# A linear-attention and feed-forward kernel on one core: its opening section in written order, and loads of k, r and v that no longer wait for one another

## The chip, the core and the metric

The kernel runs on one core of a Trainium2 chip. A core has five engines with instruction queues of their own: TensorE (PE in the profile; PEld is its loading of weights), VectorE (DVE), ScalarE (ACT), GpSimd (POOL) and SyncE (SP), which in this kernel issues nearly all DMA transfers. Engines wait for one another and for DMAs by semaphores. The metric is the device time of one execution, in microseconds (us); lower is better. A change counts as faster or slower from 2% on, which is 10.4 us here.

## The reference: what is computed

Two blocks, one after the other, in float32. The first is a recurrent attention (RWKV-5) with batch 4, 8 heads, 768 steps and head size 48; the second is a feed-forward block whose two branches are multiplied.

```python
def _attn_ref(r, k, v, w, u):
    B, H, S, D = r.shape                       # 4, 8, 768, 48
    state = np.zeros((B, H, D, D), dtype=np.float32)
    y = np.zeros_like(r)
    for t in range(S):
        kt, vt, rt = (k[:, :, t], v[:, :, t], r[:, :, t])
        cur = np.einsum('bhd,bhe->bhde', u[None] * kt, vt)
        y[:, :, t] = np.einsum('bhd,bhde->bhe', rt, state + cur)
        state = w[None, :, :, None] * state + np.einsum('bhd,bhe->bhde', kt, vt)
    return y

def _moe_ref(x, w1, w2, w3, w_out):            # x (3072, 384), d_ff 1024
    a = x @ w1
    b = x @ w2
    h = a * b @ w3
    return h @ w_out
```

w is a decay between 0.85 and 0.95 for each head and channel. The weights w1, w2, w3 and w_out arrive in float64, 8 bytes a number, and the kernel turns them into float32 itself.

## The kernel before

The sequence is cut into 6 chunks of 128 steps. A chunk of one batch entry is a *unit*; there are 24, numbered from 0. Inside a chunk the recurrence becomes matrix products, for which k and r are scaled by powers of w. A short section ahead, the *prologue*, computes those powers and a flag: if every w lies between 0.6 and 1.6, a fast arm is taken, otherwise a careful one. All engines load the flag and branch. With these inputs it is the fast arm.

In the fast arm the order of the instructions on TensorE, ScalarE, VectorE and SyncE is a written list. Its words are a letter for the step and numbers for the unit or the piece of weights:

```python
ORDER = """
kr.2 v.2 d.0 W.2 N.0 e.0 f.0 M.0 k.0 g.0 H.0 U.0 kr.3 d.1 T.0 k.1 L.0 R.0 e.1 kr.4 t.0 i.0 f.1 r.0 T.1 W.3 Q.0 p.0 A.0
M.1 h.1 j.0 S.0 t.1 d.2 R.1 k.2 m.0 r.1 R.2 kr.5 e.2 U.1 N.1 r.2 f.2 A.1 M.2 H.1 T.2 i.1 L.1 m.1 V.0 d.3 p.1 W.4 Q.1
...
"""
```

`kr.n` and `v.n` issue the loads of unit n, `W.i` that of the weight piece i. `d`, `e` and `f` form the products k*r*u and sum them; `k` scales k and r; `M`, `N`, `H`, `L` and `Q` turn a weight piece into float32, by turns on ScalarE and VectorE; `T`, `R`, `t` and `r` turn k and r on TensorE and copy them; `U` and `A` are products for the state and inside the chunk; `S`, `V` and `Y` make the output of a unit; `a`, `b`, `c` and `u` are the first layer of the feed-forward block.

The loads. k, r and v are small pieces of 192 KB, in rows of 192 bytes; a weight piece `W` has 768 KB. There are three buffers for each. Every small piece waits for the small piece two before it:

```python
small = []

def load(n, which="krv"):
    ...
    for nm, src, dst in (("k", k, krin[n % NIN][:, 0]), ("r", r, krin[n % NIN][:, 1]), ("v", v, vnat[n % NV][:, :, :D])):
        if nm in which:
            small.append(nc.sync.dma_start(out=dst, in_=src[b, :, ts, :].rearrange("h t d -> t h d")))
            if len(small) > 2:
                tc.add_manual_dep(small[-1].ins, small[-3].ins.name, ONE_AFTER_THE_OTHER, reason="few small pieces at a time")

def fetch(i, queue=nc.sync):
    if i < len(pieces):
        _, m, n = pieces[i].shape
        landed[i] = raws[i % NRAW][:, :m * n].rearrange("p (m n) -> p m n", m=m)
        queue.dma_start(out=landed[i], in_=pieces[i])
```

The prologue. Its order on the engines is chosen by a scheduler, not by the list. w is loaded twice: as one row for the flag, and by channels, in two halves, for the powers. The powers `both` have a buffer of their own, whose memory the fast arm uses again:

```python
nc.sync.dma_start(out=wrow, in_=w.rearrange("h d -> (h d)").rearrange("(o n) -> o n", o=1))
for i in range(2):
    nc.sync.dma_start(out=wucol[i * PAD:i * PAD + D], in_=w.rearrange("(p i) (d o) -> i d p o", i=2, o=1)[i])
load(0, "kr")
fetch(0)
nc.sync.dma_start(out=ub..., in_=u...)
load(0, "v")
load(1, "kr")
fetch(1)
load(1, "v")

nc.vector.tensor_reduce(ends[:, 0:1], wrow, AX.X, ALU.min)
nc.vector.tensor_reduce(ends[:, 1:2], wrow, AX.X, ALU.max)
nc.vector.tensor_scalar(ends[:, 2:3], ends[:, 0:1], W_LOW, None, ALU.is_ge)
nc.vector.scalar_tensor_tensor(flag, ends[:, 1:2], W_HIGH, ends[:, 2:3], ALU.is_le, ALU.mult)

# powers of w by doubling: wn_in, then both, on VectorE
...
for g in range(2):
    nc.vector.tensor_copy(out=both[:, g, :, T:], in_=both[:, g, :, :T])
    ps = psW.tile([P, NP, C], F32, tag="w", name=f"ps_p{g}")
    for p in range(NP):
        nc.tensor.transpose(ps[:, p, :], both[:, g, p, :], ident)
    nc.scalar.copy(out=pn_in[:, g].rearrange("t h d -> t (h d)"), in_=ps.rearrange("x p t -> x (p t)"))

inside = nc.values_load(flag[0:1, 0:1], min_val=0, max_val=1, ...)
```

First steps of the fast arm, to which the profile's line numbers 408, 411, 415 and 399 belong:

```python
def scale(n):                                   # k.n
    nc.vector.tensor_mul(krs[n % NS][:, :, :, :D], krin[n % NIN], pn[:, :, :, :D])
def rk(n):                                      # d.n
    ruk[n] = work.tile([C, H, D], F32, tag="ruk", bufs=1, name=f"ruk{n}")
    nc.vector.tensor_mul(ruk[n], krin[n % NIN][:, 0], krin[n % NIN][:, 1])
def rku(n):                                     # e.n
    nc.vector.tensor_mul(ruk[n], ruk[n], ub)
def dots(n):                                    # f.n
    nc.vector.tensor_reduce(dg[n], ruk[n], AX.X, ALU.add)
```

Of the kernel before, what the change touches and what calls it, by code (L numbers as in the profile page):

```python
# [8 lines left out]
F32 = mybir.dt.float32  # L9
# [8 lines left out]
ONE_AFTER_THE_OTHER = mybir.DependencyInfo(mybir.DependencyClass.Sync, mybir.DependencyReason.DATA)  # L18
# [5 lines left out]
kr.2 v.2 d.0 W.2 N.0 e.0 f.0 M.0 k.0 g.0 H.0 U.0 kr.3 d.1 T.0 k.1 L.0 R.0 e.1 kr.4 t.0 i.0 f.1 r.0 T.1 W.3 Q.0 p.0 A.0  # L24
M.1 h.1 j.0 S.0 t.1 d.2 R.1 k.2 m.0 r.1 R.2 kr.5 e.2 U.1 N.1 r.2 f.2 A.1 M.2 H.1 T.2 i.1 L.1 m.1 V.0 d.3 p.1 W.4 Q.1
v.3 Y.0 t.2 j.1 S.1 g.2 N.2 A.2 k.3 V.1 H.2 R.3 kr.6 Y.1 U.2 m.2 M.3 v.4 T.3 N.3 L.2 a.0.0.0 k.4 r.3 W.5 i.2 a.0.1.0
H.3 p.2 c.0.0.0 e.3 L.3 R.4 j.2 S.2 f.3 M.4 W.6 U.3 Q.3 b.0.0.0 o.4 h.3 c.0.1.0 i.3 t.3 V.2 d.4 p.3 k.5 kr.7 T.4 Y.2
e.4 A.3 v.5 r.4 x.5 S.3 t.4 b.0.1.0 m.3 o.5 y.5 j.3 M.5 V.3 u.0.0.0 u.0.1.0 U.4 f.4 Y.3 v.6 A.4 Q.2 g.4 a.0.0.1 k.6
N.5 b.0.0.1 M.6 N.6 m.4 c.0.0.1 H.6 a.0.1.1 z.5 u.0.0.1 L.6 H.5 b.0.1.1 c.0.1.1 x.6 W.9 L.5 a.0.2.2 u.0.1.1 y.6 i.4
W.8 l.5 Q.6 p.4 d.5 a.0.3.2 Q.5 c.0.2.2 kr.8 j.4 N.4 e.5 S.4 H.4 c.0.3.2 M.8 z.6 U.5 f.5 M.9 V.4 N.8 d.6 L.4 A.5 i.5  # L30
kr.9 b.0.2.2 Y.4 h.5 o.6 e.6 W.7 p.5 m.5 v.7 l.6 Q.4 b.0.3.2 j.5 u.0.2.2 N.9 k.7 U.6 f.6 A.6 x.7 g.6 S.5 k.8 y.7 V.5
d.7 M.7 a.0.4.2 m.6 v.8 kr.10 o.7 e.7 u.0.3.2 Y.5 f.7 z.7 x.8 b.0.4.2 c.0.4.2 d.8 y.8 h.7 kr.11 e.8 i.6 a.0.5.2 f.8
p.6 u.0.4.2 l.7 d.9 j.6 b.0.5.2 c.0.5.2 e.9 H.8 f.9 L.8 H.9 W.11 d.10 L.9 A.7 Q.8 W.12 U.7 u.0.5.2 a.0.6.2 N.7 i.7 H.7
p.7 k.9 L.7 a.0.7.2 j.7 kr.12 c.0.6.2 x.9 W.10 Q.9 y.9 S.6 Q.7 c.0.7.2 z.8 o.8 V.6 m.7 e.10 b.0.6.2 Y.6 g.8 v.9 N.10
N.11 S.7 M.10 f.10 M.11 u.0.6.2 z.9 V.7 o.9 H.10 b.0.7.2 l.8 d.11 Y.7 H.11 v.10 L.10 e.11 L.11 Q.10 W.13 g.9 Q.11 W.14
a.1.0.2 N.12 u.0.7.2 M.12 f.11 H.12 M.13 a.1.1.2 d.12 L.12 N.13 e.12 c.1.0.2 W.15 Q.12 M.14 H.13 N.14 L.13 b.1.0.2
H.14 c.1.1.2 W.16 Q.13 L.14 Q.14 W.17 M.15 N.15 b.1.1.2 H.15 u.1.0.2 L.15 Q.15 W.18 M.16 N.16 A.8 H.16 u.1.1.2 a.1.2.2
L.16 m.8 l.9 W.19 N.17 M.17 Q.16 H.17 M.18 b.1.2.2 N.18 c.1.2.2 H.18 L.17 L.18 Q.17 W.20 M.19 Q.18 W.21 G.0.0 N.19
G.0.1 K.0.0 u.1.2.2 U.8 H.19 a.1.3.2 K.0.1 i.8 L.19 k.10 p.8 W.22 M.20 N.20 kr.13 x.10 F.0 c.1.3.2 H.20 M.21 y.10 j.8
L.20 Q.19 W.23 M.22 Q.20 N.21 N.22 H.21 H.22 L.21 b.1.3.2 X.0 Q.21 W.24 L.22 Q.22 W.25 M.23 N.23 A.9 u.1.3.2 U.9 H.23  # L40
S.8 i.9 L.23 z.10 V.8 k.11 o.10 a.1.4.2 g.10 N.24 x.11 v.11 kr.14 Q.23 Y.8 m.9 y.11 b.1.4.2 p.9 W.26 N.25 f.12 c.1.4.2
j.9 l.10 d.13 e.13 S.9 u.1.4.2 o.11 A.10 z.11 a.1.5.2 m.10 a.1.6.2 c.1.5.2 l.11 a.1.7.2 c.1.6.2 b.1.5.2 V.9 u.1.5.2
U.10 c.1.7.2 v.12 G.1.0 i.10 Y.9 G.1.1 g.11 k.12 b.1.6.2 x.12 kr.15 p.10 f.13 y.12 K.1.0 d.14 b.1.7.2 M.24 j.10 M.25
e.14 u.1.6.2 K.1.1 H.24 S.10 H.25 L.24 z.12 A.11 u.1.7.2 o.12 U.11 Q.24 L.25 V.10 m.11 W.28 G.2.0 k.13 g.12 W.27 G.2.1
v.13 F.1 i.11 kr.16 Q.25 p.11 f.14 N.26 Y.10 j.11 l.12 d.15 K.2.0 x.13 K.2.1 e.15 y.13 N.27 G.3.0 X.1 U.12 S.11 k.14
o.13 V.11 i.12 kr.17 A.12 Y.11 x.14 G.3.1 v.14 g.13 a.2.0.2 z.13 m.12 K.3.0 f.15 y.14 p.12 d.16 G.4.0 K.3.1 e.16
b.2.0.2 j.12 K.4.0 c.2.0.2 l.13 U.13 u.2.0.2 S.12 k.15 z.14 o.14 V.12 i.13 A.13 Y.12 x.15 G.4.1 g.14 v.15 F.2 m.13
y.15 kr.18 K.4.1 f.16 l.14 d.17 M.26 e.17 M.27 H.26 p.13 H.27 L.26 j.13 S.13 L.27 W.29 Q.26 M.28 W.30 V.13 Q.27 o.15
z.15 N.28 A.14 Y.13 H.28 U.14 X.2 m.14 G.5.0 L.28 v.16 G.5.1 i.14 g.15 F.3 W.31 Q.28 N.29 k.16 M.29 f.17 kr.19 p.14
H.29 j.14 L.29 x.16 l.15 Q.29 S.14 y.16 K.5.0 N.30 d.18 X.3 F.4 K.5.1 N.31 e.18 o.16 z.16 G.6.0 X.4 G.6.1 K.6.0 F.5  # L50
M.30 K.6.1 H.30 M.31 L.30 H.31 Q.30 L.31 s.1.2.0 Q.31 s.1.2.1 F.6 s.1.0.0 X.5 s.1.2.3 s.1.1.0 s.1.3.0 s.1.1.2 s.1.3.1
s.1.1.1 s.1.3.3 s.1.3.2 s.1.0.1 s.1.0.2 s.1.0.3 s.1.2.2 G.7.0 X.6 s.1.1.3 U.15 K.7.0 G.7.1 i.15 P.0.0.0 K.7.1 k.17
p.15 F.7 x.17 kr.20 j.15 y.17 A.15 X.7 s.0.1.0 V.14 s.0.0.0 E.0.0.0 l.16 B.0 P.0.1.0 Y.14 v.17 s.0.0.1 g.16 m.15
a.2.1.2 s.0.0.3 B.1 E.0.1.0 f.18 B.2 a.2.2.2 c.2.1.2 B.3 s.0.1.2 s.0.0.2 s.0.2.0 b.2.1.2 d.19 c.2.2.2 s.0.2.2 s.0.2.1
s.0.1.1 s.0.2.3 s.0.3.0 b.2.2.2 s.0.1.3 s.0.3.1 u.2.1.2 s.0.3.3 e.19 s.0.3.2 P.0.0.2 u.2.2.2 P.0.1.2 E.0.0.2 P.0.0.3
E.0.1.2 P.0.0.4 E.0.0.3 P.0.1.3 E.0.0.4 P.0.0.5 E.0.1.3 P.0.1.5 E.0.0.6 E.0.0.5 D.0.0.0 P.0.1.4 E.0.1.6 A.16 E.0.1.4
U.16 E.0.1.5 m.16 D.0.1.0 P.0.0.6 i.16 k.18 p.16 P.0.0.1 j.16 kr.21 S.15 x.18 z.17 o.17 V.15 E.0.0.1 E.0.0.7 U.17 Y.15
a.2.3.2 i.17 g.17 y.18 v.18 k.19 D.0.0.1 kr.22 p.17 f.19 a.2.4.2 l.17 d.20 j.17 c.2.3.2 x.19 e.20 y.19 P.0.1.1 c.2.4.2
# [4 lines left out]
v.19 k.20 p.18 f.20 kr.23 x.20 l.18 a.2.6.2 c.2.5.2 j.18 y.20 d.21 e.21 b.2.5.2 c.2.6.2 a.2.7.2 u.2.5.2 s.2.1.0  # L63
# [25 lines left out]

# [4 lines left out]
def kernel(  # L94
# [86 lines left out]
    wucol = const.tile([P, NP, 1], F32)  # L181
    nc.vector.memset(wucol, 1.0)
    warm = const.tile([1, 1], F32)
    nc.vector.memset(warm, 0.0)
    nc.scalar.activation(out=warm, in_=warm, func=ABS)
# [13 lines left out]
    small = []  # L199

    def load(n, which="krv"):

        if n >= NU:
            return
        c, b = units[n]
        ts = slice(c * C, (c + 1) * C)
        for nm, src, dst in (("k", k, krin[n % NIN][:, 0]), ("r", r, krin[n % NIN][:, 1]), ("v", v, vnat[n % NV][:, :, :D])):
            if nm in which:
                small.append(nc.sync.dma_start(out=dst, in_=src[b, :, ts, :].rearrange("h t d -> t h d")))
                if len(small) > 2:  # L210
                    tc.add_manual_dep(small[-1].ins, small[-3].ins.name, ONE_AFTER_THE_OTHER, reason="few small pieces at a time")

# [19 lines left out]
    wrow = const.tile([1, DM], F32)  # L232
    ub = const.tile([P, H, D], F32)
    nc.sync.dma_start(out=wrow, in_=w.rearrange("h d -> (h d)").rearrange("(o n) -> o n", o=1))
    for i in range(2):
        nc.sync.dma_start(out=wucol[i * PAD:i * PAD + D], in_=w.rearrange("(p i) (d o) -> i d p o", i=2, o=1)[i])
    load(0, "kr")
    fetch(0)
    nc.sync.dma_start(out=ub.rearrange("t h d -> t (h d)"),
                      in_=u.rearrange("h d -> (h d)").rearrange("(o n) -> o n", o=1).to_broadcast([P, DM]))  # L240
    load(0, "v")
    load(1, "kr")
    fetch(1)
    load(1, "v")


    ends = const.tile([1, 3], F32)
    flag = const.tile([1, 1], I32)
    nc.vector.tensor_reduce(ends[:, 0:1], wrow, AX.X, ALU.min)
    nc.vector.tensor_reduce(ends[:, 1:2], wrow, AX.X, ALU.max)  # L250
    nc.vector.tensor_scalar(ends[:, 2:3], ends[:, 0:1], W_LOW, None, ALU.is_ge)
    nc.vector.scalar_tensor_tensor(flag, ends[:, 1:2], W_HIGH, ends[:, 2:3], ALU.is_le, ALU.mult)


    pn_in = const.tile([C, 2, H, PAD], F32)
    with tc.tile_pool(name="once", bufs=1) as once, tc.tile_pool(name="psW", bufs=2, space=PSUM) as psW:

        wn_in = const.tile([P, LEVELS + 1, 3 * NP, 1], F32)
        nc.vector.tensor_scalar(wn_in[:, 0, 0:NP, :], wucol, W_LOW, W_HIGH, ALU.max, ALU.min)
        for l in range(LEVELS):  # L260
            nc.vector.tensor_mul(wn_in[:, l + 1, 0:NP, :], wn_in[:, l, 0:NP, :], wn_in[:, l, 0:NP, :])
        nc.vector.reciprocal(wn_in[:, 0:LEVELS, NP:2 * NP, :], wn_in[:, 0:LEVELS, 0:NP, :])
        nc.vector.tensor_copy(out=wn_in[:, 0:LEVELS, 2 * NP:, :], in_=wn_in[:, 0:LEVELS, 0:NP, :])

        both = once.tile([P, 2, NP, C], F32)
        nc.vector.memset(both[:, 0, :, HT:HT + 1], 1.0)
        nc.vector.tensor_copy(out=both[:, 1, :, HT:HT + 1], in_=wn_in[:, 0, NP:2 * NP, :])
        bf = both.rearrange("x g p t -> x (g p) t")
# [8 lines left out]
        for g in range(2):  # L277
            nc.vector.tensor_copy(out=both[:, g, :, T:], in_=both[:, g, :, :T])
            ps = psW.tile([P, NP, C], F32, tag="w", name=f"ps_p{g}")
            for p in range(NP):  # L280
                nc.tensor.transpose(ps[:, p, :], both[:, g, p, :], ident)
            nc.scalar.copy(out=pn_in[:, g].rearrange("t h d -> t (h d)"), in_=ps.rearrange("x p t -> x (p t)"))
# [594 lines left out]
```

## Time and profile before

| | |
|---|---|
| time, median of 3 | 519.57 us (519.14 to 519.92) |
| span of the profiled execution | 517.4 us |
| TensorE busy | 492.6 us (95%) |
| VectorE, ScalarE, GpSimd busy | 278.4, 182.6, 6.0 us |
| moved by DMA | 52.72 MB, in 96865 packets, 77729 of them under 512 bytes |

The profile comes from one execution. It has a picture of the span in 40 slices, in which a digit is the busy share in tenths; groups of instructions, with the time that their engine sat idle before them and who ended that idle time; the chain of work that ended last, followed back from the end, at each step to what released it; and the instructions in order of time. Names such as `raw<-in_moe_w_dram` say what is written and what is read: `raw` are the weight pieces, `krin` holds k and r of a unit, `vnat` v, `krs` the scaled k and r, `ps_p` the turned powers, `tt` the turned r, `ps_a` and `ps_b` products. `L408` is a line of the kernel. Matmuls overlap in TensorE's pipeline, and the ends shown for them are modelled.

### The profile page before, as it was taken

To read this page: it belongs to the slowest core of one execution; us is meant where nothing else is said; L and a number is where in the kernel's file an instruction comes from. 1 tells how busy PE (TensorE), PEld (TensorE's weight loads), DVE (VectorE), ACT (ScalarE), POOL (GpSimd) and SP (SyncE) were. 2 spreads that over 40 slices of the span, in tenths; PEclk is the share of its full clock that TensorE was granted. 3 is DMA by queue.
4 is the path that set the end of the run, shared out by engine and by line. 5 is a ranking of instruction groups with operands and counts; after the bars stand their busy time and mean duration, and the time that the engine had idled before them with its cause. 6 is when DMAs were issued, how large, how long until landed. Compare 5 with 4: busy or idle time off the path is not lost.

```text
span 517.4 us, 12199 instructions
## 1 busy us (share of the span) xinstructions
PE 492.6 (95%) x5192; PEld 321.8 (62%) x5192; DVE 278.4 (54%) x587; ACT 182.6 (35%) x455; POOL 6.0 (1%) x23
## 2 busy tenths in 40 slices
PE   1969999999999999999999999999999999999996
PEld 1757544445466566759797477564874754855486
DVE  6888798788475686575424542376321314211342
ACT  3677546766467483411302200340051410001100
POOL 4000000000000000000000000000000000000000
PEclk9999999999999999999999999999999999999999
DMA  7788887668537592301601301220041100000001
GB/s 204 165 220 241 210 219 209 168 232 252 157 94 198 153 232 69 75 3 50 182 32 45 95 0 46 63 79 32 0 129 42 48 1 0 7 24 16 1 16 67
DMA packets 96865, 52.72 MB, mean 102 GB/s; under 512 B 77729, under 2 KB 88226, under 8 KB 96802
## 3 DMA queue, kind: packets, MB, share of 16 engines
q1 hardware_dynamic: 96802, 51.86, 36.9%
q8 instruction: 43, 0.70, 0.6%
q14 instruction: 20, 0.16, 0.1%
HBM read 39.65 MB, written 12.19 MB: 100 GB/s over the span
## 4 chain that ended last, share of the span: by engine, by line
PE 75%; DMA 13%; ACT 4%; DVE 4%; SPq 2%; issue 1%; ACTq 0%; DVEq 0%
PE ps_a L659 20%; PE ps_b L659 19%; DMA raw<-in_moe_w_dram 6%; PE ps_w L387 6%; DMA tt<-scratch 3%; PE ps_s4b L716 3%; PE ps_a12b L716 3%; PE ps_a22t L716 3%; PE ps_s2t L716 3%; PE ps_s1t L716 3%; PE ps_s3t L716 3%; PE ps_a11b L716 3%; PE ps_y L619 2%; SPq L480 2%; PE ps_a L519 2%; PE ps_y L633 2%
## 5 line engine op out<-in xcount | busy, mean ns | idle before, releaser
L659 PE MATMUL ps_a<-xT,w 128*128 128x512 f32 (+1 forms) x300 | 131.4, 581 | 0.8 <-ACT xT L641 0.7
L659 PE MATMUL ps_b<-xT,w 128*128 128x512 f32 (+1 forms) x300 | 131.1, 578 | 0.9 <-DVE abt L670 0.5
L659 PEld LDWEIGHTS ps_b<-xT,w 128*128 128x128 f32 x300 | 55.9, 190 | 63.7 <-issue 56.9
L670 DVE TENSOR_TENSOR abt<-ps_b,a 128x512 f32<-128x512 f32 (+1 forms) x50 | 33.3, 666 | 110.2 <-PE ps_b L659 110.1
L659 PEld LDWEIGHTS ps_a<-xT,w 128*128 128x128 f32 x300 | 55.3, 190 | 57.8 <-issue 53.6
L665 ACT COPY a<-ps_a 128x512 f32<-128x512 f32 (+1 forms) x50 | 28.2, 566 | 127.1 <-PE ps_a L659 123.3
L544 ACT COPY wide<-st 64x192 f32<-64x192 f32 x88 | 30.5, 347 | 56.5 <-PE ps_y L619 27.6
L426 ACT ACTIVATE AT<-same,dg 128x64 f32<-128x64 f32 x160 | 40.4, 336 | 6.2 <-DVE dg L415 3.8
L387 PE MATMUL ps_w<-wo,w3T 128*128 128x384 f32 x128 | 42.5, 487 | 0.0
L387 PEld LDWEIGHTS ps_w<-wo,w3T 128*128 128x128 f32 x128 | 23.9, 190 | 15.7 <-ACT wide L544 0.2
L361 ACT ACTIVATE t<-raw 128x512 uint32<-128x512 uint32 (+2 forms) x32 | 22.4, 705 | 7.2 <-DVE w3n L357 5.0
L619 PEld LDWEIGHTS ps_y<-tt,wide 128*32 128x32 f32 x1056 | 16.5, 111 | 11.2 <-issue 5.6
L399 DVE TENSOR_TENSOR krs<-krin,pn_in 128x768 f32<-128x768 f32 x24 | 22.8, 949 | 0.0
L619 PE MATMUL ps_y<-tt,wide 128*32 128x64 f32 x1056 | 21.1, 223 | 1.7 <-ACT xT L641 1.0
L633 PE MATMUL ps_y<-AT,vnat 64*64 64x64 f32 x1152 | 22.3, 223 | 0.0
L468 DVE STREAM_TRANSPOSE tr<-krs 128x768 f32<-128x768 f32 x19 | 18.5, 973 | 6.5 <-DMA scratch<-tr 6.4
L512 PE MATMUL ps_a<-vnat,krs 64*64 64x48 f32 x704 | 16.7, 227 | 5.1 <-DVE krs L399 3.3
L633 PEld LDWEIGHTS ps_y<-AT,vnat 64*64 64x64 f32 x1152 | 19.3, 136 | 3.1 <-issue 1.4
L485 ACT COPY kT<-tt 128x512 f32<-128x512 f32 x19 | 11.7, 617 | 26.9 <-DMA tt<-scratch 23.8
L547 DVE COPY_PREDICATED AT<-later,ps_a 128x512 f32<-128x512 int32 x24 | 17.4, 726 | 5.6 <-PE ps_a L519 3.0
L519 PEld LDWEIGHTS ps_a<-tt,kT 64*64 64x64 f32 x768 | 14.9, 141 | 8.8 <-issue 4.3
L512 PEld LDWEIGHTS ps_a<-vnat,krs 64*64 64x64 f32 x704 | 14.3, 142 | 9.4 <-issue 8.8
(102 smaller groups left out, 564.2 us busy)
## 6 DMA issues: line engine op xcount, KB each, us to landing
raw<-in_moe_w_dram SPq DMA_DIRECT2D x16, 512.0 KB, 4.9
scratch<-tr SPq DMA_DIRECT2D x19, 384.0 KB, 3.4
raw<-in_moe_w_dram SPq DMA_DIRECT2D x8, 768.0 KB, 6.4
tt<-scratch SPq DMA_DIRECT2D x38, 128.0 KB, 3.2
krin<-in_k_dram SPq DMA_DIRECT2D x24, 192.0 KB, 3.3
krin<-in_r_dram SPq DMA_DIRECT2D x24, 192.0 KB, 3.4
vnat<-in_v_dram SPq DMA_DIRECT2D x24, 192.0 KB, 4.0
raw<-in_moe_w_out_dram SPq DMA_DIRECT2D x8, 384.0 KB, 4.4
```

What stands on the lines that cost most here:

```text
L387: nc.tensor.matmul(ps, lhsT=w3T[j][:, kc, :], rhs=wo[kc], start=(kc == 0), stop=(kc == KF - 1))
L399: nc.vector.tensor_mul(krs[n % NS][:, :, :, :D], kr, pn[:, :, :, :D])
L426: nc.scalar.activation(out=AT[n][:, i, p, :], in_=same, func=COPY, scale=dg[n][:, h:h + 1])
L512: nc.tensor.matmul(added(n)[rows(i), a, p, :], lhsT=kk[rows(a), 2 * p + i, :], rhs=vnat[n % NV][rows(a), 2 * p + i, 0:D], start=True, stop ...
L519: nc.tensor.matmul(upper(n)[rows(a), i, p, :], lhsT=kT[n][rows(i), p, rows(a)], rhs=rT[n][rows(i), p, 2 * a:2 * a + 2], start=True, stop=True)
L544: nc.scalar.copy(out=wide[a][n % 2][rows(i), :, i * D:(i + 1) * D], in_=st[units[n][1]][rows(i)])
L619: nc.tensor.matmul(yt[n][g * Q:(g + 1) * Q, a, q, :], lhsT=wide[a][n % 2][:, p, j * Q:(j + 1) * Q], rhs=rw[:, p, 2 * a:2 * a + 2] if fast ...
L633: nc.tensor.matmul(yt[n][rows(g), a, q, :], lhsT=vv[rows(a), x:x + PAD], rhs=AT[n][rows(a), h % 2, h // 2, :], start=(a, g) not in seen, s ...
L659: nc.tensor.matmul(ps, lhsT=(w1 if x == "a" else w2)[:, z, q, js], rhs=xT[c][:, q, ts], start=(q == 0), stop=(q == KM - 1))
L665: nc.scalar.copy(out=a, in_=ps)
L670: nc.vector.tensor_mul(abt[c, j][:, parts_of_tokens[part]], factor["b", c, j, part], factor["sa", c, j, part])
L716: nc.tensor.matmul(ps, lhsT=of[:, m * C:(m + 1) * C], rhs=w34[:, KH * (x == 1) + j, :DH] if x < 2 else made[b][:, j, :], start=(j == 0), s ...
```

## The change

The prologue is written in the order in which the engines are to run it, and reorganised:

- w is loaded once, by channels; its two halves are issued by SyncE and by ScalarE. The load of v goes ahead of that of u.
- The flag is no longer made from the smallest and largest w. Each w is compared with its value held between the bounds; a product with ones on TensorE counts the differences, and VectorE sums the four counts and tests for zero, at the end of the prologue.
- The powers `both` lie in the third weight buffer, `raws[2]`, in place of a buffer of their own. The third weight piece, W.2, which goes into that buffer, follows after them.
- One of the two copies of powers moves from VectorE to ScalarE.
- 14 products of a matrix of ones keep TensorE busy while it has nothing else to do; their result is not used.
- The loads of k, r and v lose the wait for the piece two before. In the list, `kr.n` becomes `kk.n rr.n`, the same two loads in the same order.

```diff
-ONE_AFTER_THE_OTHER = mybir.DependencyInfo(mybir.DependencyClass.Sync, mybir.DependencyReason.DATA)
...
-kr.2 v.2 d.0 W.2 N.0 e.0 f.0 M.0 k.0 g.0 H.0 U.0 kr.3 d.1 T.0 k.1 L.0 R.0 e.1 kr.4 t.0 i.0 f.1 r.0 T.1 W.3 Q.0 p.0 A.0
+kk.2 rr.2 v.2 d.0 W.2 N.0 e.0 f.0 M.0 k.0 g.0 H.0 U.0 kk.3 rr.3 d.1 T.0 k.1 L.0 R.0 e.1 kk.4 rr.4 t.0 i.0 f.1 r.0 T.1
...
-                small.append(nc.sync.dma_start(out=dst, in_=src[b, :, ts, :].rearrange("h t d -> t h d")))
-                if len(small) > 2:
-                    tc.add_manual_dep(small[-1].ins, small[-3].ins.name, ONE_AFTER_THE_OTHER, reason="few small pieces at a time")
+                nc.sync.dma_start(out=dst, in_=src[b, :, ts, :].rearrange("h t d -> t h d"))
...
-    nc.sync.dma_start(out=wrow, in_=w.rearrange("h d -> (h d)").rearrange("(o n) -> o n", o=1))
-    for i in range(2):
-        nc.sync.dma_start(out=wucol[i * PAD:i * PAD + D], in_=w.rearrange("(p i) (d o) -> i d p o", i=2, o=1)[i])
-    load(0, "kr")
-    fetch(0)
-    nc.sync.dma_start(out=ub.rearrange("t h d -> t (h d)"),
-                      in_=u.rearrange("h d -> (h d)").rearrange("(o n) -> o n", o=1).to_broadcast([P, DM]))
-    load(0, "v")
...
-    nc.vector.tensor_reduce(ends[:, 0:1], wrow, AX.X, ALU.min)
-    nc.vector.tensor_reduce(ends[:, 1:2], wrow, AX.X, ALU.max)
-    nc.vector.tensor_scalar(ends[:, 2:3], ends[:, 0:1], W_LOW, None, ALU.is_ge)
-    nc.vector.scalar_tensor_tensor(flag, ends[:, 1:2], W_HIGH, ends[:, 2:3], ALU.is_le, ALU.mult)
...
+    with tc.manual_schedule(engines={PE, ACT, DVE, SP}), tc.tile_pool(name="psW", bufs=2, space=PSUM) as psW:
+        nc.vector.memset(wucol, 1.0)
+        for i, queue in enumerate((nc.sync, nc.scalar)):
+            queue.dma_start(out=wucol[i * PAD:i * PAD + D], in_=w.rearrange("(p i) (d o) -> i d p o", i=2, o=1)[i])
+        load(0, "kr")
+        fetch(0)
+        load(0, "v")
+        nc.sync.dma_start(out=ub.rearrange("t h d -> t (h d)"),
+                          in_=u.rearrange("h d -> (h d)").rearrange("(o n) -> o n", o=1).to_broadcast([P, DM]))
+        load(1, "kr")
+        fetch(1)
+        load(1, "v")
+
+        busy = pn_in[:, 0].rearrange("t h d -> t (h d)")[:, :C]
+        nc.vector.memset(busy, 1.0)
...
+        keep_busy(14)
...
+        both = raws[2].bitcast(F32)[:, :2 * NP * C].rearrange("x (g p t) -> x g p t", g=2, p=NP)
...
             nc.vector.tensor_mul(wn_in[:, l + 1, 0:NP, :], wn_in[:, l, 0:NP, :], wn_in[:, l, 0:NP, :])
+            if l == 0:
+                nc.vector.tensor_tensor(outs[:, 0:NP], wn_in[:, 0, 0:NP, 0], wucol[:, :, 0], ALU.not_equal)
+                ps_out = psW.tile([1, NP], F32, tag="out", bufs=1, name="ps_out")
+                nc.tensor.matmul(ps_out, lhsT=outs[:, NP:NP + 1], rhs=outs[:, 0:NP], start=True, stop=True)
...
-        both = once.tile([P, 2, NP, C], F32)
...
+        nc.vector.tensor_copy(out=both[:, 0, :, T:], in_=both[:, 0, :, :T])
+        nc.scalar.copy(out=both[:, 1, :, T:], in_=both[:, 1, :, :T])
+        nc.vector.tensor_reduce(outs[0:1, NP + 1:], ps_out, AX.X, ALU.add)
+        nc.vector.tensor_scalar(flag, outs[0:1, NP + 1:], 0.0, None, ALU.is_equal)
         for g in range(2):
-            nc.vector.tensor_copy(out=both[:, g, :, T:], in_=both[:, g, :, :T])
             ps = psW.tile([P, NP, C], F32, tag="w", name=f"ps_p{g}")
```

## The prediction

> **What bounds the kernel now.** I read the page's slices first, then the busy time by stage, then the chain that ended last, and last the instructions of the first 40 us in order of time. The slices (one is 12.9 us):
>
> ```profile
> PE   1969999999999999999999999999999999999996
> ...
> DMA  7788887668537592301601301220041100000001
> ```
>
> TensorE is full from the fourth slice to the last but one; the DMA engines are nearly full only in the first seven. So the kernel is TensorE-bound except at its head. The stages put numbers on that (us, then busy us and instruction counts of PE, PEld, DVE, ACT and POOL, the granted clock, the DMA share, GB/s):
>
> ```profile
> 0.00:9.60 9.60, 1.94 (x8) 1.57 (x8) 4.96 (x30) 2.10 (x4) 6.04 (x23) 1.00 0.71 177
> 9.60:26.00 16.40, 12.15 (x224) 9.81 (x224) 14.22 (x26) 10.75 (x23) 0.00 (x0) 1.00 0.78 188
> 26.00:39.00 13.00, 9.11 (x221) 7.57 (x222) 11.05 (x21) 10.27 (x25) 0.00 (x0) 1.00 0.88 221
> 39.00:48.00 9.00, 8.33 (x238) 6.83 (x237) 7.52 (x14) 5.99 (x18) 0.00 (x0) 1.00 0.91 255
> ...
> 58.00:104.00 46.00, 45.05 (x631) 23.50 (x631) 40.49 (x82) 28.00 (x72) 0.00 (x0) 1.00 0.76 198
> ...
> 200.00:400.00 200.00, 199.51 (x1747) 137.54 (x1745) 92.69 (x204) 46.16 (x130) 0.00 (x0) 1.00 0.20 56
> ```
>
> TensorE idles 7.66 + 4.25 + 3.89 = 15.8 us of the first 39, and 24.8 us of the whole span, of which 4.1 lie in the drain after 510 us. From 39 to 510 us there are 4.9 us in all. Whatever the change does must be read from the first 39 us: if the list of instructions gets to that point sooner by x, the end comes sooner by about x.
>
> What sets the pace up to there is in the chain that ended last (start, length, what):
>
> ```profile
> 4.82 5.47 DMA vnat<-in_v_dram
> ...
> 10.35 4.13 DMA krin<-in_r_dram
> ...
> 14.50 2.64 DMA krin<-in_k_dram
> ...
> 17.57 6.42 DMA raw<-in_moe_w_dram
> ...
> 25.81 6.45 DMA raw<-in_moe_w_dram
> ...
> 38.35 6.32 DMA raw<-in_moe_w_dram
> ```
>
> Each of the first three starts within 0.1 us of the landing of the piece two places before it: that is the wait "few small pieces at a time". It holds the one SyncE queue, so the third weight piece behind it is issued only at 17.57 us. VectorE, 84 to 87% busy in each stage from 9.6 to 48 us, shows what this costs it:
>
> ```profile
> 9.63 0.56 DVE L408 TENSOR_TENSOR ruk<-krin 128x384 f32<-128x384 f32 x1 [1.98 <-PE ps_p L281]
> ...
> 14.60 0.56 DVE L408 TENSOR_TENSOR ruk<-krin 128x384 f32<-128x384 f32 x1 [1.16 <-DMA krin<-in_r_dram]
> ...
> 25.49 0.56 DVE L408 TENSOR_TENSOR ruk<-krin 128x384 f32<-128x384 f32 x1 [0.59 <-DMA krin<-in_r_dram]
> ...
> 32.28 0.56 DVE L354 TENSOR_SCALAR t<-raw 128x768 uint32<-128x768 uint32 x1 [1.17 <-DMA raw<-in_moe_w_dram]
> ```
>
> The last numbers are its idle time before the instruction and who ended it: once TensorE's transposes of the powers, three times a load.
>
> **What the Trainium skill says.** "DMA: Bandwidth & Descriptors", section "Why small descriptors are slow (HBM only)": each packet carries a fixed cost. The trace agrees: while the 192-byte pieces of k and r run (3.5 to 5.5 us) about 200 GB/s flow, while a weight piece or u runs about 360. Same page, "Latency and other measured facts": loading a register from memory costs at least about 600 ns. Here ScalarE's last copy of the prologue is dispatched at 9.57 us and its first instruction past the branch starts at 10.26, so load and branch together fit in 0.69 us. Same page, "Issuing engines are not separate DMA queues": two issuing engines save only issue time. No run shows it yet. "TensorE: Matmul & The Clock Gate", Part 1: some 3.4 us of activity should bring the full clock. The trace agrees only in part: four transposes take 1.11 us at 13.9 us and 0.66 at 29.0, so the array is at half clock and then at full, but it stays at half for 12 us of work with gaps of at most 0.7 us. So small products and transposes may hardly count as activity.
>
> **The change part by part.** The order of instructions past the branch is the same on TensorE, ScalarE, VectorE and SyncE; "kk, rr" in the list is what "kr" was, and the new list words are not used. What differs there are waits: VectorE's first instruction no longer waits for TensorE, the third weight piece waits for the prologue's readers of its buffer, and every wait of a small load for the one two before it is gone. The wait of each DMA for the one eight before it stays.
>
> 1. *Prologue on VectorE.* Its chain starts when w has landed, at 3.58 us. The first half of w is issued at 1.21 us behind the row of w, the second at 1.61. Now the row is gone and the halves go out side by side: done about 0.65 us sooner, chain start 2.9. The chain lasted to 7.64, or 4.06 us. One comparison comes in (0.15), one of two copies of 0.25 goes to ScalarE, and the flag's sum and test come at the end (two tiny instructions, 0.4 with their waits). Flag at 2.9 + 4.06 + 0.15 - 0.25 + 0.4 = 7.25. With 0.7 for load and branch VectorE enters the list at 7.95 instead of 9.63: 1.7 us.
>
> 2. *First loads.* Service times from the rates: a 197 KB small piece 1.0 us, a 786 KB weight piece 2.2, u 0.55; landing 1.0 after the last byte (checked on the first v: data from 3.5, 5.75 us of pieces, 9.25 + 1.0 against 10.29 seen). k starts 0.73 earlier, data from 2.75. In the new order k, r, weights, v, u, k, r, weights, v, then k, r, v, weights: u lands at 9.5, the second r at 11.5, the third r at 16.7, the third weight piece at 19.9 (seen now: 23.99). After it k, r, k, r: the fourth r at 21.9 (now 25.46), the fourth weight piece at 26.1 (now 32.25). Of the 1.7 us only 1.1 survives, because the product with u (10.57 now) waits for u, which has moved behind v.
>
> 3. *VectorE down the list.* k and r of the second unit are there before it needs them (11.5 against 12.3): the 1.16 goes. The fourth r (needed at 22.6): 0.59 goes. The fourth weight piece (needed at 28.2): 1.17 goes. Sum 1.1 + 1.16 + 0.59 + 1.17 = 4.0 us at 32 us.
>
> 4. *Beside the path.* ScalarE's waits for weights (1.41, 2.54 and 1.59 us) and TensorE's for v at 37.37 us (1.68) shrink too, but lie mostly beside VectorE's line; with the clock below I give them 0.5 us.
>
> 5. *Dummy products.* Eight cold transposes took 1.94 us, so 14 take 3.4 us, from 1.1 to 4.5, while TensorE has nothing to do. The transposes of the powers then may take 1.0 instead of 1.94, off the path since VectorE no longer waits for them. After 4 us of nearly nothing the clock may well fall back.
>
> Sum: 4.0 + 0.5 = 4.5 us, to be carried to the end by a TensorE that idles 0.65 us in all from 200 to 510. 519.6 - 4.5 = 515.1; I say 515.0.
>
> **A second count.** By DMA time: 39 us at shares 0.71, 0.78 and 0.88 are 31 us of transfers. At 0.95 from 2 us on they end at 34.7: 4.3 us sooner. The two counts agree, so neither VectorE nor DMA would let much more through.
>
> **Rivals.** (a) *Loads crowd out weights.* With up to eight transfers open, a weight piece queues behind five small ones, and the limit was presumably put in because that cost something. For it: share 0.91 from 39 to 48 us leaves little. Against: in order of issue nothing is served later than now. Time 518 to 521. (b) *The gain is taken back at 52 to 58 us.* VectorE waits there 2.78 us for a copy behind a 4.94 us wait of ScalarE for the turned rows' round trip through memory. If that trip, behind the same weights, doesn't move forward, TensorE starves: 517 to 518. (c) *The flag on the path.* It was ready at 4 us and now ends the prologue, and all engines wait for it. If its chain takes 1.5 us more than I count, the start gives nothing: 516.5. (d) *Warm clock throughout.* TensorE's half-clock work from 12.8 to 26 us would halve (some 6 us); ScalarE's waits for it there are 1.15 and 1.23 us, VectorE's 0.34: 513 or a little less.
>
> **Range and chances.** The most there is to take is 15.8 us of idle plus 6 of half clock, less about 10 of unavoidable start: 12 us. 2% is 10.4, so nearly all of it would be needed: 4%. A loss of 10.4 us needs a new stall of a kind the trace doesn't show: 2%. Eight times in ten between 512.0 and 519.0.
>
> **What would show it.** VectorE's first instruction of the list near 8.0 us, the product with u near 9.5; no wait for k or r of 0.5 us or more; third and fourth weight pieces landing near 20 and 26 us; DMA share 0.9 or more from 10 to 39 us; TensorE from 39 us on a copy of now, shifted by 4 to 5 us. I am wrong if weight pieces land no sooner, if the idle before the turned rows' copy grows by what was won, or if the clock is full from 12 us on and the gain above 7 us.

## The result, and the profile after

The changed kernel takes 510.44 us (median of 4, 510.0 to 511.5), beside 519.36 us for the kernel before (median of 4, 517.46 to 519.92): a ratio of 0.984, 95% interval 0.981 to 0.987. That is 8.9 us where 4.5 were expected, and 1.6%, less than the 2% from which a change counts. The range of 512 to 519 us does not hold it.

The page of the kernel after, TensorE's slices, the granted clock and the DMA engines:

```profile
PE   4789999999999999999999999999999999999996
...
PEclk9899999999999999999999999999999999999999
DMA  7997986768358680304403101230050100000001
```

TensorE is full from the fourth slice on, as before. Its first slice, where the dummy products are, shows 4 in place of 1 and its third 8 in place of 6, but its second 7 in place of 9; the DMA engines are busier in the second and third. By stage (us, then busy us and counts of PE, PEld, DVE, ACT and POOL, the granted clock, DMA share, GB/s):

```profile
0.00:9.60 9.60, 5.91 (x38) 5.48 (x38) 5.24 (x32) 3.47 (x6) 6.03 (x23) 1.00 0.74 182
9.60:26.00 16.40, 10.48 (x269) 8.62 (x273) 14.87 (x27) 11.51 (x26) 0.00 (x0) 0.79 0.97 235
26.00:39.00 13.00, 11.69 (x300) 9.76 (x293) 12.00 (x21) 10.75 (x26) 0.00 (x0) 1.00 1.00 262
39.00:48.00 9.00, 9.00 (x143) 7.29 (x143) 8.56 (x16) 7.07 (x17) 0.00 (x0) 1.00 0.78 210
...
200.00:400.00 200.00, 199.69 (x1902) 137.54 (x1904) 87.79 (x190) 49.20 (x141) 0.00 (x0) 1.00 0.21 58
```

The DMA share went from 0.78 to 0.97 between 9.6 and 26 us and from 0.88 to 1.00 up to 39 us: the loads no longer wait for one another. TensorE works through 300 matmul instructions between 26 and 39 us, where it had 221. (One float32 product shows as two matmul instructions and two weight loads: the 14 dummy products as 28 and 28.) VectorE's instructions that the prediction followed (start, length, what; idle before it in brackets):

```profile
8.22 0.56 DVE L413 TENSOR_TENSOR ruk<-krin 128x384 f32<-128x384 f32 x1 [0.85 <-DVE flag L282]
...
10.33 0.56 DVE L416 TENSOR_TENSOR ruk<-ruk,ub 128x384 f32<-128x384 f32 x1 [0.73 <-DMA ub<-in_u_dram]
...
13.13 0.55 DVE L413 TENSOR_TENSOR ruk<-krin 128x384 f32<-128x384 f32 x1
...
23.77 0.54 DVE L413 TENSOR_TENSOR ruk<-krin 128x384 f32<-128x384 f32 x1
...
29.27 0.55 DVE L359 TENSOR_SCALAR t<-raw 128x768 uint32<-128x768 uint32 x1
```

The waits of 1.16, 0.59 and 1.17 us before the third, fourth and fifth are gone. Lines of the kernel after are 5 higher than before for the same step.

Where the 9 us were won is seen best on TensorE, whose order is the same in both kernels. The start of one and the same product, before minus after:

| at (us, before) | 14.4 | 21.1 | 25.1 | 32.2 | 35.1 | 40.0 | 50.2 | 58.1 | 90.1 | 130 | 164 | 174 | 186 | 250 | 400 |
|---|---|---|---|---|---|---|---|---|---|---|---|---|---|---|---|
| gained (us) | 0.24 | 0.87 | 2.31 | 1.74 | 3.07 | 3.51 | 4.51 | 5.27 | 6.07 | 5.62 | 6.31 | 7.04 | 8.63 | 8.63 | 9.13 |

At 40 us, where the prediction had its whole sum of 4.5 us, 3.5 stand; 4.5 are reached at 50 us, and another 4.6 come after that. TensorE's own waits in that later part, from 39 us to the end of the list (who waits for whom, us in total, times, longest), first before:

```profile
PE ps_a L519 <- ACT kT L485: 0.9, 2, 0.6
PE ps_a L659 <- ACT xT L641: 0.7, 1, 0.7
PE ps_y L619 <- ACT wide L544: 0.5, 2, 0.3
...
PE ps_a L519 <- DVE st L535: 0.5, 1, 0.5
PE ps_a L519 <- issue: 0.4, 1, 0.4
```

and after, where these three are all that is left:

```profile
PE ps_b L664 <- ACT a L670: 0.7, 1, 0.7
PE ps_w3T L382 <- DVE w3n L369: 0.5, 1, 0.5
PE ps_a L517 <- DVE AT L552: 0.2, 1, 0.2
```

Before, there are nine such rows, 4.5 us in all; after, these three, 1.4 us. The first line is the wait for turned rows that come back from memory; the last one shown, "issue", is a wait for nothing that the profile shows, and becomes important further on.

### The profile page after: what moved, and what is told of

The parts are those of the page before. It is cut to its first block, busy times and chain, and to the rows that moved or that the text cites. A ratio compares the mean times of both kernels' runs of the same rounds, so it can differ in the third digit from the quotient of the medians.

```text
span 508.3 us, 12255 instructions
## 1 busy us (share of the span) xinstructions
PE 491.7 (97%) x5222; PEld 323.3 (64%) x5222; DVE 277.3 (55%) x587; ACT 183.2 (36%) x456; POOL 6.0 (1%) x23
## 4 chain that ended last, share of the span: by engine, by line
PE 88%; DMA 5%; DVE 2%; SPq 2%; ACT 1%; issue 1%; DVEq 0%; ACTq 0%
PE ps_b L664 23%; PE ps_a L664 22%; PE ps_w L392 8%; PE ps_y L638 3%; PE ps_y L624 3%; PE ps_s4b L721 3%; PE ps_a12b L721 3%; PE ps_a11b L721 3%; PE ps_a22t L721 3%; PE ps_s1t L721 3%; PE ps_s3t L721 3%; PE ps_s2t L721 3%; PE ps_a L524 3%; PE ps_a L517 2%; PE ps_w3T L382 2%; DMA krin<-in_r_dram 1%
## 5 line engine op out<-in xcount | busy, mean ns | idle before, releaser
L624 PE MATMUL ps_y<-tt,wide 128*32 128x64 f32 x1056 | 19.7, 221 | 1.5 <-ACT xT L646 1.5
L490 ACT COPY kT<-tt 128x512 f32<-128x512 f32 x19 | 11.7, 618 | 21.1 <-DMA tt<-scratch 17.8
L540 DVE TENSOR_TENSOR st<-ps_a,st 128x192 f32<-128x192 f32 x40 | 13.9, 347 | 8.6 <-PE ps_a L517 4.9
```

Source lines behind the costliest of these rows:

```text
L624: nc.tensor.matmul(yt[n][g * Q:(g + 1) * Q, a, q, :], lhsT=wide[a][n % 2][:, p, j * Q:(j + 1) * Q], rhs=rw[:, p, 2 * a:2 * a + 2] if fast ...
```

## The experiments

Each batch was timed beside runs of the kernel before on the same chip; ratios are to those, with 95% intervals. e1 to e4 ran beside 519.94 us, e5 to e8 beside 520.52, e9 to e12 beside 518.92, e13 to e15 beside 521.44. Two theories at first: W, the waits of the small loads carry the gain, early and late; P, the prologue does.

### The waits and the prologue apart (e1 to e4)

e1 is the kernel before without the waits:

```diff
-                if len(small) > 2:
-                    tc.add_manual_dep(small[-1].ins, small[-3].ins.name, ONE_AFTER_THE_OTHER, ...)
```

> The kernel before, with only the wait of each small load for the one two before it taken out; the prologue stays as it was. Theory W (the waits held SyncE's queue, in the opening and again later): it gives most of the 9 us, about 7.5: 512 us (511 to 513.5). Rival P (the rewritten prologue, with its earlier entry and the early full clock, gives more than a third): 514.5 us or more.

515.27 us, ratio 0.992 (0.989 to 0.994).

e2 is the kernel after with all the waits put back:

```diff
+                small.append(nc.sync.dma_start(out=dst, in_=...))
+                if len(small) > 2:
+                    tc.add_manual_dep(small[-1].ins, small[-3].ins.name, ONE_AFTER_THE_OTHER, ...)
```

> The changed kernel with the wait of each small load for the one two before it put back. Theory W: only the prologue's share is left, 1 to 1.5 us: 518 us (517 to 519.2). Rival P: 515 us or less.

517.76 us, ratio 0.996 (0.993 to 0.999). By the ratios, on 519.94 us, the waits alone are worth 4.4 us, the prologue alone 2.1 and both 8.4: some 2 us more than the sum, though each interval is 1.3 us or more to either side. Neither W nor P has room for that: e1 lies above W's range and in P's, e2 in W's and above P's.

e3 puts the waits back for units 13 to 23 alone (`if len(small) > 2 and n >= 13:`), e4 for units 0 to 12 (`n < 13`).

> The changed kernel with the waits put back for units 13 and up alone, whose loads start at 116 us in the kernel before. If the gain seen between 164 and 183 us comes from the waits of that stage, about 3 us are lost: 513.4 us (512.5 to 514.2). If the gain was all made in the opening and only showed later: 510.4 us, as the changed kernel.

512.25 us, ratio 0.987 (0.980 to 0.993): between the two forecasts, and the interval reaches both.

> The changed kernel with the waits put back for units 0 to 12 alone. Theory W, both stages count by themselves: 5 to 5.5 us are lost, 515.7 us (514.5 to 516.5), and this loss and that of the run with the waits from unit 13 on add up to the loss with all of them. If the opening alone matters: as with all waits, 518 us.

516.39 us, ratio 0.994 (0.992 to 0.996). The waits that matter most are those of the first half. SyncE's own waits for v, in the kernel before between 150 and 185 us and in e3 between 145 and 180 (us in total, times, longest):

```profile
SPq L209 <- DMA vnat<-in_v_dram: 5.8, 2, 4.6
```

```profile
SPq L203 <- DMA vnat<-in_v_dram: 6.0, 2, 4.2
```

e3 has this wait of over 4 us again, and still TensorE gains from 5.7 to 7.5 us between 130 and 186 us, where the kernel after goes from 5.6 to 8.6. So in these executions 1.2 of the 3.0 us of late growth belong to the late waits.

### The parts of the prologue (e5 to e8)

The sum that does not add up pointed to something in the prologue that matters only once the loads are free. Theory C: the dummy products, by the early full clock. e5 takes them out:

```diff
-        keep_busy(14)
+        keep_busy(0)
```

> The changed kernel without its 14 dummy products. Theory C (the clock decides a good part of the opening): TensorE is at half clock for longer after 12.6 us, in some executions up to 25 us or more, so 513 us (511.5 to 515.5) and a spread of over 2.5 us between executions, where the changed kernel has 1.5. Theory W (waits alone; the dummies' clock was lost again at 10.8 us): 510.4 us (509.8 to 511.2).

515.27 us, ratio 0.989 (0.985 to 0.992): more is lost than C had forecast, and in the prediction the dummy products were worth nothing. e6 gives the powers a buffer of their own again, e7 loads u ahead of v, e8 adds 14 more dummy products at the head of TensorE's list:

```diff
-        both = raws[2].bitcast(F32)[:, :2 * NP * C].rearrange("x (g p t) -> x g p t", g=2, p=NP)
+        both = once0.tile([P, 2, NP, C], F32)
```

```diff
+        nc.sync.dma_start(out=ub..., in_=u...)
         load(0, "v")
-        nc.sync.dma_start(out=ub..., in_=u...)
```

```diff
-U.0 kk.3 rr.3
+Z.14 U.0 kk.3 rr.3
```

> The changed kernel with the powers in a buffer of their own again, whose memory the fast arm reuses. VectorE's first list instruction then waits for TensorE's transposes, which end at 8.35 us: it starts 0.2 to 0.3 us later, but the product with u waits for u until 10.33 anyway. Theory W and C: no difference, 510.4 us (509.6 to 511.2). If the entry into the list counts: 511.5 us or more. If the third weight piece was held back by the powers: 509.5 us or less.

> The changed kernel with the load of u ahead of that of v again. VectorE's product with u starts near 9.6 us in place of 10.33. If the start of TensorE's list work follows: 0.5 to 0.7 us less, 509.8 us (509.2 to 510.2). If later loads set the pace: 510.4 us (510 to 511).

> The changed kernel with 14 more dummy products at the head of TensorE's list, in the 4.2 us that it idles before its first product at 12.6 us. Theory C: the clock stays full at 10.8 us, the 5.1 us of TensorE work from 12.6 to 17.75, which stand in the chain that ended last, become some 3 us, and 0.8 to 1.5 us of it reach the end: 509.3 us (508.7 to 509.8). Theory W: 510.4 us.

e6: 512.43 us, ratio 0.983 (0.979 to 0.986). That is above 511.5, as if the entry into the list counted; but the kernel before is slower in this batch too, and by the ratio e6 is the same as the kernel after. The buffer is worth nothing that shows. e7: 511.18 us, 0.981 (0.978 to 0.984), no difference to be told from after, though the product with u starts at 9.17 us in place of 10.33. e8: 515.73 us, 0.989 (0.986 to 0.993), 3.3 and 4.6 us above e6 and e7, though the trace's clock records have TensorE at full clock from 5.1 to 18.8 us. That went against C: more warming gave as bad a time as none (e5 is 2.8 and 4.1 us above e6 and e7).

The largest piece that e5 lost is one pause. TensorE in e5 (start, length, what, idle before it and who ended it):

```profile
27.73 0.32 PE L517 MATMUL ps_a<-vnat,krs 64*64 64x48 f32 x4
30.96 0.96 PE L517 MATMUL ps_a<-vnat,krs 64*64 64x48 f32 x28 [2.92 <-issue]
```

and the same group in the kernel after:

```profile
27.82 0.68 PE L517 MATMUL ps_a<-vnat,krs 64*64 64x48 f32 x32
```

In e5 TensorE stops for 2.92 us after 4 of 32 matmul instructions of one group, which wait for nothing. VectorE stands behind it, in e5 and then in the kernel after:

```profile
32.04 0.73 DVE L552 COPY_PREDICATED AT<-later,ps_a 128x512 f32<-128x512 int32 x1 [4.08 <-PE ps_a L517]
```

```profile
28.64 0.74 DVE L552 COPY_PREDICATED AT<-later,ps_a 128x512 f32<-128x512 int32 x1 [0.59 <-PE ps_a L517]
```

3.40 us behind at this instruction, and at 40 us TensorE of e5 is still 3.4 us behind that of the kernel after. e1, the kernel before without waits, has a pause of 2.07 us in the same group of products. In its later course e5 stops once more in this way, where the kernel after does not:

```profile
172.59 0.57 PE L524 MATMUL ps_a<-tt,kT 64*64 64x64 f32 x21 [1.16 <-issue]
```

What could stop an engine that waits for nothing? The page's list of queues has two lines of the kind "instruction"; the larger one (packets, MB, share of 16 engines) is the same before and after:

```profile
q8 instruction: 43, 0.70, 0.6%
```

These 43 packets have 16,384 bytes each. The Trainium skill says in "Trainium Architecture — The Big Picture", section "The software stack", that an instruction has 64 bytes; as an estimate from that figure, a packet holds 256. TensorE's 5222 matmul instructions, 5222 weight loads and 93 others come to 245 for each of 43. The packets are spread over the whole span of the execution. So theory F: a few more TensorE instructions ahead of the list move the places at which its next 256 instructions are needed; where such a place falls early in a group while the DMA engines are full, TensorE waits.

### The number of instructions and the work in them (e9 to e12)

e9 keeps the 14 dummy products but makes them tiny, e10 adds 14 tiny ones to the 14 large ones, e11 is e1 with 14 tiny ones, e12 is e7 with tiny ones:

```diff
-                nc.tensor.matmul(ps_busy, lhsT=busy, rhs=busy, start=True, stop=True)
+                nc.tensor.matmul(ps_busy[:8, :8], lhsT=busy[:, :8], rhs=busy[:, :8], start=True, stop=True)
```

> The 14 dummy products shrink to 8x8 columns: as many TensorE instructions as in the kernel after (56), next to no work. Theory C (the dummy products help by an early full clock): the time is that of the kernel without dummies, 515.3 +/- 1. Theory F (they help because 56 more instructions move the places at which TensorE's 16 KB instruction fetches fall, away from the products with the old values at 28 us): 510.5 +/- 1, and no pause inside a group of products near 28 to 31 us.

> The 14 large dummy products as in the kernel after, and then 14 of 8x8 columns: the early clock of the kernel after, but 56 more instructions ahead of the list, as many as in the run with 14 more large products at the list's head. Theory C: 510.5 +/- 1. Theory F: as slow as the run with 14 more large ones, 514 to 516, with a pause at a fetch inside a group of products between 29 and 46 us.

> The kernel before without the waits of the small loads (515.3 alone), with 14 products of 8x8 columns in its written-out start: 56 more instructions, no warming. Theory F: 511 to 512.5, the pause at 29 to 31 us gone. Theory C: 515.3 +/- 1.

> The kernel after with u ahead of v and the dummy products of 8x8 columns. Theory F: as u-first alone, 510 to 511.5. Theory C: about 515.

| run | dummy products | us | ratio, interval |
|---|---|---|---|
| e9 | 14 tiny | 510.61 | 0.982 (0.978 to 0.986) |
| e10 | 14 large, 14 tiny | 515.50 | 0.991 (0.988 to 0.995) |
| e11 | 14 tiny, prologue of before | 512.76 | 0.985 (0.981 to 0.989) |
| e12 | 14 tiny, u first | 511.99 | 0.984 (0.980 to 0.988) |

The tiny ones in e9 (ns least, median, most; first and last start us):

```profile
L250 PE MATMUL ps_busy<-pn_in x28: 170/172/181, 1.2 to 1.8; 128*8 128x8 f32 x28
```

They are over by 2 us, and the trace has no full clock before 16.4 us; yet e9 is as fast as the kernel after. e10 has the early full clock of the kernel after, and is 4.9 us slower than e9 by 56 instructions that take under a microsecond. C is out: what the dummy products bring is their number. The trace of e10 has five pauses without a named wait, 4.2 us in all, of the 5.4 us that its profiled execution is longer than that of e9, which has one of 0.26 us. The longest is at 42 us (shown below); the last:

```profile
180.78 0.31 PE L518 MATMUL ps_a<-vnat,krs 64*64 64x48 f32 x2 [1.04 <-issue]
```

e11 lands 0.3 us outside F's forecast and 2.5 from C's: the pause of e1 is gone, and TensorE waits once for 2.0 us for a load of v instead. e12 lies 0.5 us above F's forecast and 3 below C's. From e11 to e9 the rest of the prologue adds 2.1 us, with intervals that overlap.

### A whole period (e13 to e15)

Open was whether the fetches or a plain count is behind it. 64 products are 256 instructions, one whole packet; 7 and 21 lie between the values tried.

```diff
-        keep_busy(14)
+        keep_busy(64)
```

> 64 dummy products of 8x8 columns in place of 14 large ones: 256 TensorE instructions, one whole 16 KB fetch if an instruction is 64 bytes. They would end near 4.6 us, ahead of the transposes at 7.2 us. Theory F (places of the fetches): as with none, 515.3 +/- 1, with a pause inside the products with the old values at 28 to 31 us. Theory G (any instructions ahead of the list help or hurt by their number alone, without a period): unlike none, and no such pause there.

> 7 dummy products of 8x8 columns: 28 instructions, half way between none (515.3) and 14 (510.6). Theory F: any pause falls 28 instructions earlier in the work than with none; the time lies between 510 and 516, with no sum to foresee it from. Theory G: about 513.

> 21 dummy products of 8x8 columns: between 14 (510.6) and 28 (515.5). Theory F: between 510 and 516; if the place of 14 is merely one of several good ones, near 511. Theory G: about 513.

e13: 513.36 us, ratio 0.986 (0.982 to 0.990). e14: 514.96 us, 0.988 (0.983 to 0.992). e15: 513.59 us, 0.986 (0.982 to 0.989). By their times these settle little: e13 is 2 us faster than F had it, outside F's range, and its interval overlaps those of e5 and e9; for e14 and e15 F's range of 6 us excluded next to nothing, and e15 is near G's 513. The traces settle it. TensorE in e13, and in e10:

```profile
30.16 0.45 PE L517 MATMUL ps_a<-vnat,krs 64*64 64x48 f32 x4
32.38 0.67 PE L517 MATMUL ps_a<-vnat,krs 64*64 64x48 f32 x28 [1.76 <-issue]
```

```profile
41.51 0.54 PE L525 MATMUL ps_a<-tt,kT 64*64 64x64 f32 x22
43.61 0.44 PE L525 MATMUL ps_a<-tt,kT 64*64 64x64 f32 x10 [1.57 <-issue]
```

With 64 products the pause is back at the very place where e5 has it, after 4 of 32. And with 256 instructions more there is one packet of instructions more than in the kernel after:

```profile
q8 instruction: 44, 0.72, 0.6%
```

I numbered the records of TensorE in order (weight loads, products, and those of its sequencer) and noted the number at which each pause without a named wait ends, with the 16 KB packet nearest to it:

| run | dummy products | pause (us) | at record | packet (us) |
|---|---|---|---|---|
| e5 | 0 | 28.04 to 30.96 | 705 | 28.31 to 29.40 |
| e1 | 0 | 28.95 to 31.02 | 705 | 28.34 to 29.46 |
| e14 | 7 | 27.92 to 31.24 | 705 | 28.69 to 29.58 |
| e13 | 64 | 30.61 to 32.37 | 961 = 705 + 256 | 29.90 to 31.09 |
| e13 | 64 | 44.01 to 44.70 | 1473 = 705 + 3 x 256 | 42.31 to 43.23 |
| e10 | 28 | 42.05 to 43.61 | 1473 | 40.95 to 42.13 |
| e8 | 28 | 44.16 to 45.38 | 1473 | 42.64 to 43.89 |
| e15 | 21 | 44.49 to 45.48 | 1473 | 42.92 to 44.10 |
| after | 14 | none over 0.3 | | |
| e9 | 14 | 26.45 to 26.72 | 705 | 23.22 to 25.12 |

The table stops at 60 us; the pauses do not. From 12 to 505 us the traces of all 17 kernels have 23 pauses of over 0.25 us without a named wait, and every one ends at such a record, a whole number of 256s away from 705, whatever the work there; each time TensorE goes on 1.2 to 1.7 us after a packet has ended. F holds. The kernel before has one too, 0.42 us at 174.5 us (record 4801 = 705 + 16 x 256); the kernel after has none.

How much of a run's time this explains differs. The pauses come to 4.1 of the 5.7 us by which the profiled execution of e5 is longer than that of the kernel after, but only to 2.9 of 5.8 us in e8 and 2.5 of 7.3 in e15: what else these lose was not tested.

Why a packet is late is less clear. In e5, e1, e14 and e13 it begins within about 0.3 us of the landing of the weight piece issued at 22 to 24 us (landed at 28.49, 28.63, 28.38 and 29.82), 5 to 7 us after TensorE went past the place 256 records earlier (22.97, 22.64, 22.28 and 22.89). In the kernel after and in e9 it begins 1.3 us after that place, well before that piece has landed. That it queues behind the weight piece is a guess from these times, not shown: e14 passed the place at 22.28 us and the kernel after at 22.76, both ahead of the end of the piece's issue (22.99 and 23.27), yet only the packet of e14 was late. No run here beats the kernel after by more than the intervals.

## Why the prediction was wrong, by its steps

**Step 1, right in kind.** The flag was ready at 7.37 us (forecast 7.25) and VectorE entered the list at 8.22 (7.95): 1.41 of the 1.7 us. w landed at 3.16, not 2.9.

**Step 2, right.** The second r landed at 11.64 us (11.5), the third at 17.12 (16.7), the third weight piece at 21.39 (19.9; before 23.99), the fourth at 28.67 (26.1; before 32.25), u at 10.23 (9.5). Pieces came a little later than the rates gave, and the product with u gained only 0.24 us, not 1.1.

**Step 3, right in kind, short in size.** All three waits are gone, but VectorE is 3.01 us ahead at the instruction at 32.28 us, where 4.0 were forecast, because of the product with u. It is 3.3 us ahead at 38 and 4.50 at 49.6. That this is the very sum is partly luck: TensorE won 1.0 us of it after 40 us, in a stage that the prediction had left out. What step 4 brought by itself was not measured.

**Step 5 failed.** "14 take 3.4 us, from 1.1 to 4.5, while TensorE has nothing to do", "off the path", "the clock may well fall back". The products took 4.7 us, from 1.15 to 5.88; the rest came true: in the kernel after the clock records show full clock from 3.98 to 10.81 us, half to 17.63, and full from there. The edges lie 6.83 us apart, twice the 3.4 us window that the Trainium skill gives in "TensorE: Matmul & The Clock Gate", Part 1, section "What's actually happening". But the step took the products' work and clock for all that they do. Their 56 instructions are worth 2.8 to 4.1 us (e5 against e6 and e7, one batch), and 56 more cost 4.9 (e10 against e9, one batch), because they shift TensorE's instruction fetches. Without them the sum of 4.5 us is not reached: in e5 TensorE has 1.1 us at 50 us. So the early sum came out only because the products happened to keep away a pause that nobody had counted; the step from 4.5 to 8.9 us is the next failure.

**The carrying to the end failed.** "From 39 to 510 us there are 4.9 us in all. Whatever the change does must be read from the first 39 us." The 4.9 us were counted and then taken as out of reach. 3.3 of them were won: TensorE's idle time from 39 us to 501 is 1.5 us; the rest of the late gain lies inside what the profile counts as busy. The gain grows from 4.5 to 9.1 us: 0.8 at 58 us, 0.8 up to 90, less 0.5 to 130, 3.0 between 130 and 186, 0.5 later. Why each of these waits goes is only partly settled. Between 130 and 186 us TensorE of the kernel before idles 1.9 us, and that of the kernel after, in the same work, not at all; 0.4 us of it is the instruction pause at 174.5 us. e3 gives the late waits of loads 1.2 of the 3.0 us; what takes the rest stays open.

The two failures have opposite signs in e5, whose 515.27 us happens to be the prediction's 515.0: the early pause takes 3.4 us from the gain, and the later stages give some back.

**Rivals.** (a) Loads crowding out weights: no, weight pieces land 2.6 and 3.6 us sooner and the share from 39 to 48 us is 0.78. (b) Gain taken back at 52 to 58 us: the opposite, VectorE's stall there fell from 2.78 to 0.85 us. (c) The flag: 0.12 us later than forecast. (d) Warm clock throughout: half true. The gain was above 7 us as (d) had it, but TensorE was at half clock from 10.8 to 17.6 us. From there on it was at full clock, which the kernel before reaches only at 25.42 us. (The stages of before show 1.00 ahead of that because its trace has no clock record there.) What this earlier full clock is worth after 17.6 us was not separated from the waits: every traced run without the early waits has it before 19 us. Before that it is worth little: e8, at full clock up to 18.8 us, is 1.7 us ahead of the kernel after at 17.6 us and has lost all of it by 22 us, as TensorE waits for VectorE's scaled k and r:

```profile
PE ps_rT L451 <- DVE krs L404: 2.0, 1, 2.0
```

The second count by DMA time, 4.3 us, was an estimate for the stage up to 39 us; TensorE had 3.5 there.

## What to carry to other kernels

When a change adds or removes instructions of the engine that bounds the kernel, look in the trace for pauses with no named wait, number the engine's records there, and see whether they lie a fixed number apart: a time that hangs on where instruction fetches fall is luck that the next edit can undo, and a handful of idle instructions shows it cheaply. Two changes that do not add up are a reason to look for such a third cause. And idle time that is counted in late stages is an amount to be won, to be given a chance of its own in the range, not left out because the head is where the change acts.

## What the hardware showed that I had not expected

- TensorE stopped 23 times in these 17 traces, for 0.26 to 3.3 us, with no wait that the profile names: always at a record that is a whole number of 256s away from the others, and always until 1.2 to 1.7 us after a 16 KB packet of instructions had ended. The DMA engines need not be full for it: around the 0.7 us pause of e15 at 281 us their share is 0.34. Not every such place costs: the kernel before has no pause at record 705.
- 56 instructions that keep an idle TensorE for 0.9 us change the time of the whole by 3 to 5 us, for better (0 to 14 products) or worse (14 to 28).
- Full clock before 10.8 us was worth nothing that these runs can measure: 510.61 us without it, 510.44 with it.
